# Attention tails of two head pairs: their products with v as 64 more columns of the neighbouring units' products

## The chip, the core and the metric

One core of a Trainium2 chip runs the kernel. The metric is the device time of one launch in microseconds (us), as the median over runs. The engines that matter are TensorE (PE, with its weight loads shown as PEld), VectorE (DVE), ScalarE (ACT), GpSimd (POOL) and SyncE (SP, which issues the DMAs).

## The reference

Inputs: q, k, v of 4 batches x 8 heads x 576 positions x 64, all float32. Rotary embedding is applied to q and k, then ordinary softmax attention:

```
scores = scale * q_rot @ k_rot^T          # 576 x 576 per head
attn   = exp(scores - rowmax) / (rowsum + 1e-9)
out    = attn @ v                         # 576 x 64 per head
```

The heads' outputs are laid side by side (4 x 576 x 512) and go through two feed-forward layers. The first mixes each row with the one before it, takes `relu(xk @ w_k)`, squares it, multiplies by `w_v` and gates with a sigmoid of `xr @ w_r`. The second takes `relu(x @ w_in)`, normalises one half, multiplies it with a 576 x 576 spatial matrix, gates the other half and multiplies by `w_out`.

## The kernel before

**Pairs, units and tails.** Two heads form a pair i, stacked on the 128 partitions (head 0 on partitions 0 to 63, head 1 on 64 to 127). There are 16 pairs, 4 per batch. The 576 queries of a pair are four chunks c of 128 and a rest of 64. A unit m is one pass of scores, softmax and transposes. Two pairs (a group g) make nine units: k = 0 to 3 are chunks 0 to 3 of the pair 2g, k = 5 to 8 the chunks of the pair 2g+1, and k = 4 is the tail: the last 64 queries of both pairs at once, with both heads of a pair stacked on the partitions. So the tails are the units 4, 13, 22, 31, 40, 49, 58 and 67 of 72.

**One unit.** `scores` writes two PSUM tiles (L337 for the first batch in float32, L329 and, for tails, L326 afterwards in three float32r terms). `top` takes the row maximum on DVE (L341), `expo` the exponential and the row sum on ACT (L346), `total` (L350, ACT) and `norm` (L353, DVE) the reciprocal of the sum. The scores of unit m+1 wait for both exponentials of unit m, since there is one set of score tiles.

**Turns.** For the products with v the weights must lie with the keys on the partitions. `turn(n)` transposes on PE with the identity: n = 0 and 1 are 512 keys each of the two heads (L382), n = 2 is the last 64 keys of both (L384) and, as a second tile, the reciprocals spread over 64 columns by `spread` (L357, ACT; L385, PE). `take(n)` copies the result from PSUM into the tile pt (L395; n = 0 and 1 on ACT, n = 2 on DVE).

**Products with v.** Two units in a row share a pt of 256 columns, a "duo". `values` multiplies them with v (L408): five key chunks x two heads, the heads in the left and right 64 columns of the array. `gather` multiplies the result with the turned reciprocals into the rows xt of the pair (L421, DVE).

**Tails before.** A tail has a duo of its own. `scaled` (DVE) multiplies the exponentials with the reciprocals (L363), and copies the last keys into a tile pe (L365). The turns of a tail wait for it (L374 for the 512 keys, L378 for pe). `values` then makes twenty products of 64 columns, ten for each pair, and two copies on DVE (L419) put the result into xt.

**The rest around it.** Of each finished batch, `feed` makes the products with w_k (mk, L506) and w_v (mv, L545), in twelve-matmul pieces, while the next batch's units run; each mv result is copied by ACT to a tile vs (L551) and stored by a DMA. During the first 18 units there is no finished batch. Weights are unpacked by DVE, ACT and POOL (L156 to L174) alongside. After the last unit the rest of the feed and the later layers follow (L681, L745).

**Order.** All this is entered as steps with an engine, a cost, predecessors and a rank. `Plan.order` builds one list per engine from these numbers and `emit` issues the instructions in that order, so each engine runs a fixed queue:

```
t, s = min((x for x in ready if x[0] <= soon), key=lambda x: (x[1].rank - ..., x[0]))
if best is None or t < best[0]:
    best = t, s
```

SP's queue, too, is such a list: the loads of v (L294), q and k (L246), weights (L151) and the stores. Buffers are counted by constants: VB tiles of v, PTB of pt, VSB of vs.

Of the kernel before, what the change touches and what calls it, by code (L numbers as in the profile page):

```python
# [7 lines left out]
F32 = mybir.dt.float32  # L8
# [4 lines left out]
ALU = mybir.AluOpType  # L13
# [3 lines left out]
B, H, S, D = 4, 8, 576, 64  # L17
# [7 lines left out]
NFIRST = 2  # L25
EXACT = NP
WB, GB, WB2, GB2 = 3, 2, 3, 2
RAW, ROT, VB, PFB, PTB, XTS = 2, 4, 3, 3, 2, 6
KB, RLB, VSB = 4, 2, 2
EARLY, EVERY = 24, 2.9  # L30
WAIT, SWITCH, BONUS = 0.3, 0.1, 0.0
SIDES = slice(0, HALF), slice(HALF, S)
HEAD = slice(0, 64), slice(64, 128)
# [17 lines left out]
class Plan:  # L51
# [5 lines left out]
    def add(self, eng, us, fn, deps=(), rank=0.0, after=0.12, take=None, give=None, port=False, kind=None):  # L57
        s = Step(eng, us, fn, deps, rank, after, take, give, port, kind)
        self.steps.append(s)
        return s  # L60
# [44 lines left out]
def body(ctx: ExitStack, tc, qp, kp, vp, cs, mu_k, mu_r, w_k, w_v, w_r, w_in, w_sp, b_sp, w_out, out):  # L105
    nc = tc.nc
# [10 lines left out]
    at = att.enter_context(tc.tile_pool(name="att", bufs=1, side="right"))  # L117
# [10 lines left out]
    ident = const.tile([128, 128], F32, name="ident")  # L128
# [77 lines left out]
    add = plan.add  # L206

    def which(m):
        g, w = divmod(m, 9)
        return [(2 * g, 4), (2 * g + 1, 4)] if w == 4 else [(2 * g + w // 5, w % 5 if w < 4 else w - 5)]  # L210

    ropes, vloads, exps, turned, valued, xdone, stored = {}, {}, {}, {}, {}, {}, {}
    qk, vt, xt = {}, {}, {}
# [89 lines left out]
    units, scored, duos, freed = {}, {}, {}, {}  # L303

    def unit(m):
        w = which(m)
        tail = len(w) == 2
        st = units[m] = {}
        g, k = divmod(m, 9)
        part = 0 if tail else (k - (k > 4)) % 2  # L310
        duo = duos.setdefault(5 * g + (k // 2 if k < 4 else 2 if tail else 3 + (k - 5) // 2), {"ev": [], "n": 0})
        duo["n"] = 5 * g + (k // 2 if k < 4 else 2 if tail else 3 + (k - 5) // 2)

        def scores(halves=(0, 1)):
            if 0 in halves:
# [37 lines left out]
            nc.vector.reciprocal(st["sm"][:, 3, :], st["sm"][:, 2, :])  # L353

        def spread():
            st["r"] = at.tile([128, 2, D], F32, tag="rb", bufs=3, name=f"rb{m}")
            nc.scalar.copy(st["r"], st["sm"][:, 3, :].unsqueeze(2).to_broadcast([128, 2, D]))  # L357

        def scaled(u):
            p, r = st["p"][:, u, :], st["sm"][:, 3, u:u + 1]  # L360
            if u == 0:
                st["e"] = at.tile([128, 2, 128], F32, tag="pe", name=f"pe{m}")
            nc.vector.tensor_scalar(p, p, r, None, op0=ALU.mult)  # L363
            for j in range(2):
                nc.vector.tensor_copy(st["e"][:, u, HEAD[j]], p[:, 512 - 512 * j:576 - 512 * j])  # L365

        def turn(n, slot):
            pt = st["t", n] = ps_t.tile([128, 4, 128], F32, tag=f"t{slot}", name=f"t{m}_{n}")
            p = st["p"]
            if tail and n < 2:  # L370
                for u in range(2):
                    for c in range(4):
                        k = 64 * n + 128 * c
                        nc.tensor.transpose(pt.rearrange("p c (h q) -> p (c h) q", h=2)[:, 4 * u + c, :],  # L374
                                            p[HEAD[n], u, k:k + 128], ident[HEAD[n], HEAD[n]])
            elif tail:
                for u in range(2):
                    nc.tensor.transpose(pt[:, u, :], st["e"][:, u, :], ident)  # L378
            elif n < 2:
                for c in range(4):  # L380
                    k = 64 * n + 128 * c
                    nc.tensor.transpose(pt[:, c, :], p[:, n, k:k + 128], ident)  # L382
            else:
                nc.tensor.transpose(pt[:, 0, :], p.rearrange("p a b -> p (a b)")[:, 512:640], ident)  # L384
                nc.tensor.transpose(pt[:, 1, :], st["r"].rearrange("p a b -> p (a b)"), ident)  # L385

        def take(n, eng):
            if "pt" not in duo:
                duo["pt"] = at.tile([128, 10, 256], F32, tag="pt", bufs=PTB, name=f"pt{m}")
            x = st["t", n] if n < 2 else st["t", n][:, 0:2, :]  # L390
            if tail and n < 2:
                o, x = duo["pt"][:, 0:8, HEAD[n]], x.rearrange("p c (h q) -> p (c h) q", h=2)
            else:
                o = duo["pt"][:, 4 * n:min(4 * n + 4, 10), 128 * part:128 * part + 128]
            nc.scalar.copy(o, x) if eng == "ACT" else nc.vector.tensor_copy(o, x)  # L395

        def values(slot):
            pv = duo["v"] = ps_m.tile([128, 512], F32, tag=f"m{slot}", name=f"v{m}")
            pt = duo["pt"]
            for u, (i, _) in enumerate(w):  # L400
                v = vt[i]
                for c in range(5):
                    for j in range(2):
                        if tail:
                            o, a = pv[HEAD[j], 64 * u:64 * u + 64], pt[:, 4 * u + c if c < 4 else 8 + u, HEAD[j]]
                        else:
                            o, a = pv[HEAD[j], 0:256], pt[:, 4 * j + c if c < 4 else 8, :]
                        nc.tensor.matmul(o, v[:, 4 * j + c if c < 4 else 8 + j, :], a, start=c == 0, stop=c == 4)  # L408

        def rows(i):  # L410
            if i not in xt:
                xt[i] = moe.tile([128, S + 1], F32, tag="xt", bufs=XTS, name=f"xt{i}")
                nc.gpsimd.memset(xt[i][:, 0:1], 0.0)
            return xt[i]

        def gather(u=0):
            i, c = w[u]
            if tail:
                nc.vector.tensor_copy(rows(i)[:, 513:577], duo["v"][:, 64 * u:64 * u + 64])  # L419
            else:  # L420
                nc.vector.tensor_tensor(rows(i)[:, 128 * c - 127:129 + 128 * c], duo["v"][:, 0:256], duo["pt"][:, 9, :],  # L421
                                        op=ALU.mult)

        def store(i):
            b, p = divmod(i, NP)
# [9 lines left out]
                             m - 0.5)  # L435
        t = add("ACT", 0.2, total, [exps[m, 1]], m - 0.3)
        nm = add("DVE", 0.17, norm, [t], m - 0.3)
        if tail:
            sc = [add("DVE", 0.9, lambda u=u: scaled(u), [nm, turned.get((m - 9, 2))], m - 0.25, port=True) for u in range(2)]
            ready = [sc] * 3  # L440
        else:
            ready = [[exps[m, 0]], [exps[m, 1]], [add("ACT", 0.26, spread, [nm], m - 0.3)]]
        ev = duo["ev"]
        for n in range(3):
            turned[m, n] = add("PE", (0.44, 0.44, 0.22)[n], lambda slot, n=n: turn(n, slot), ready[n], m + 0.1 * n, take="t", kind="t")
            eng = ("ACT", "ACT", "DVE")[n]
            ev.append(add(eng, (0.59, 0.59, 0.42)[n], lambda n=n, eng=eng: take(n, eng),
                          [turned[m, n]] + freed.get(duo["n"] - PTB, []), m - 0.2, give=turned[m, n]))
        if tail or part:
            v = add("PE", 1.1 if tail else 2.2, values, ev + [vloads[i] for i, _ in w], m + 0.9, take="m", kind="v")  # L450
            for u, (i, c) in enumerate(w):
                valued[i] = v
                xdone[i, c] = add("DVE", 0.2 if tail else 0.42, lambda u=u: gather(u), [v] + mixed.get(i - XTS, []), m + 0.5,
                                  give=v if u + 1 == len(w) else None)
                freed.setdefault(duo["n"], []).append(xdone[i, c])
        if m % 9 in (4, 8):
            i = 2 * (m // 9) + (m % 9 == 8)
            stored[i] = add("SP", 0.4, lambda: store(i), [xdone[i, c] for c in (1, 3, 4)], m + 1, 3)

    mixed, kept, mo = {}, {}, {}  # L460
# [122 lines left out]
    for c in range(16):  # L583
        k = c < 8
# [5 lines left out]
    for m in range(NU):  # L590
        for i, _ in which(m):
            while i not in ropes:
                prep(len(vloads))
        unit(m)
        for n, args in enumerate(early):
            if m == EARLY + int(EVERY * n):
                weight_steps(weight_early(*args), m + 12, [scored[m]])
        for i in range(B * NP):
            if i not in ropes and i >= ROT // 2 and max(which_last(i - ROT // 2)) <= m:
                prep(i)  # L600
        if m % 18 == 17:
            if m == NU - 1:
                second["close"] = close = add("SP", 0.0, lambda: open_second(), [x for x in plan.steps if x not in fed], 74, 0.1)
            n = len(plan.steps)
            for h in range(2):
                feed(m // 18, h)
            fed.update(plan.steps[n:])
# [294 lines left out]
```

## Time and profile before

| | |
|---|---|
| median of 3 runs | 787.35 us (787.33 to 789.11) |
| the profiled execution | 788.41 us, span 786.3 us |
| mean granted TensorE clock | 0.989 |
| PE busy | 750.9 us (96%) |
| DVE busy | 492.2 us (63%) |
| ACT busy | 459.0 us (58%) |

The attention units run from about 7 to 460 us of the span, the rest of the kernel behind them. A busy PE is not PE at its peak, so the order of work and the waits are read from the chain of waits and the timeline.

### The profile page before, as it was taken

To read this page: it belongs to the slowest core of one execution; us is meant where nothing else is said; L and a number is where in the kernel's file an instruction comes from. 1 tells how busy PE (TensorE), PEld (TensorE's weight loads), DVE (VectorE), ACT (ScalarE), POOL (GpSimd) and SP (SyncE) were. 2 spreads that over 40 slices of the span, in tenths; PEclk is the share of its full clock that TensorE was granted. 3 is DMA by queue.
4 is the path that set the end of the run, shared out by engine and by line. 5 is a ranking of instruction groups with operands and counts; after the bars stand their busy time and mean duration, and the time that the engine had idled before them with its cause. 6 is when DMAs were issued, how large, how long until landed. Compare 5 with 4: busy or idle time off the path is not lost.

```text
span 786.3 us, 14710 instructions
## 1 busy us (share of the span) xinstructions
PE 750.9 (96%) x5904; PEld 662.4 (84%) x5904; DVE 492.2 (63%) x937; ACT 459.0 (58%) x1037; POOL 110.6 (14%) x132
## 2 busy tenths in 40 slices
PE   4888899899999999999999998999999999999997
PEld 2555568689888888888888797998989999998997
DVE  5978998788877977977956526336553342635111
ACT  3678797677877877778876645335432432533211
POOL 1332133302111111112011100002010000101000
PEclk9989999799999999999999999999999999999999
DMA  8354432242551362352431147163201212010101
GB/s 307 119 169 146 127 118 76 90 152 99 165 173 69 140 190 77 124 178 82 134 112 55 58 156 290 46 208 116 77 15 46 76 31 91 16 31 1 61 2 60
DMA packets 35269, 84.14 MB, mean 107 GB/s; under 512 B 4545, under 2 KB 10433, under 8 KB 35202
## 3 DMA queue, kind: packets, MB, share of 16 engines
q1 hardware_dynamic: 34658, 82.63, 31.6%
q8 instruction: 46, 0.75, 0.4%
q10 hardware_dynamic: 544, 0.59, 0.2%
q14 instruction: 21, 0.17, 0.1%
HBM read 60.65 MB, written 22.55 MB: 106 GB/s over the span
## 4 chain that ended last, share of the span: by engine, by line
PE 90%; ACT 4%; DVE 3%; DMA 2%; issue 1%; SPq 1%; ACTq 0%; DVEq 0%
PE mv L545 13%; PE v L408 11%; PE mk L506 11%; PE t L382 9%; PE sp L681 8%; PE u L681 7%; PE r L681 6%; PE hv L745 6%; PE o L681 6%; PE s L329 6%; PE s L337 3%; ACT pf L346 2%; PE s L326 1%; ACT pt L395 1%; DMA wi<-wd 1%; PE t L385 1%
## 5 line engine op out<-in xcount | busy, mean ns | idle before, releaser
L341 DVE TENSOR_REDUCE sm<-s 128x1 f32<-128x576 f32 x144 | 106.4, 750 | 32.3 <-PE s L329 23.4
L346 ACT ACTIVATE pf<-s,sm 128x576 f32<-128x576 f32 x144 | 106.7, 743 | 15.1 <-DVE sm L341 14.2
L506 PE MATMUL mk<-x,wk 128*128 128x288 f32 x768 | 113.4, 300 | 1.3 <-ACT rl L513 1.3
L545 PE MATMUL mv<-kh,wv 128*128 128x288 f32 x512 | 113.4, 304 | 1.2 <-ACT kh L520 1.2
L395 ACT COPY pt<-t 128x512 f32<-128x512 f32 x144 | 83.3, 583 | 47.2 <-PE t L382 38.8
L506 PEld LDWEIGHTS mk<-x,wk 128*128 128x128 f32 x768 | 103.4, 188 | 3.0 <-ACT rl L513 1.5
L382 PE MATMUL t<-ident,pf 128*128 128x128 f32 x512 | 84.1, 288 | 15.6 <-ACT pf L346 15.6
L408 PE MATMUL v<-pt,vt 128*64 128x256 f32 (+1 forms) x960 | 93.9, 338 | 0.4 <-DVE pt L395 0.4
L382 PEld LDWEIGHTS t<-ident,pf 128*128 128x128 f32 x512 | 58.0, 143 | 38.9 <-ACT pf L346 17.1
L545 PEld LDWEIGHTS mv<-kh,wv 128*128 128x128 f32 x512 | 85.4, 190 | 5.1 <-issue 3.6
L408 PEld LDWEIGHTS v<-pt,vt 128*64 128x64 f32 x960 | 56.5, 142 | 28.9 <-issue 7.4
L545 PE MATMUL mv<-kl,wv 128*128 128x288 f32 x256 | 76.3, 298 | 0.6 <-DVE kl L524 0.6
L681 PE MATMUL sp<-ws,vn 128*128 128x288 f32 x384 | 53.9, 295 | 0.0
L681 PE MATMUL o<-g,wo 128*128 128x288 f32 x384 | 52.9, 296 | 0.5 <-ACT os L804 0.5
L681 PEld LDWEIGHTS sp<-ws,vn 128*128 128x128 f32 x384 | 52.4, 188 | 0.7
L681 PEld LDWEIGHTS o<-g,wo 128*128 128x128 f32 x384 | 51.7, 188 | 1.4 <-ACT os L804 1.2
L681 PE MATMUL r<-xr,wr 128*128 128x288 f32 x384 | 52.4, 295 | 0.0
L681 PEld LDWEIGHTS r<-xr,wr 128*128 128x128 f32 x384 | 51.7, 188 | 0.3
L681 PE MATMUL u<-x,wi 128*128 128x288 f32 x384 | 52.0, 296 | 0.0
L681 PEld LDWEIGHTS u<-x,wi 128*128 128x128 f32 x384 | 51.6, 188 | 0.3
L545 PEld LDWEIGHTS mv<-kl,wv 128*128 128x128 f32 x256 | 48.8, 191 | 1.2 <-DVE kl L524 1.2
L249 DVE TENSOR_TENSOR raw<-raw,cst 128x1152 f32<-128x1152 f32 (+1 forms) x34 | 44.7, 1316 | 5.3 <-DMA raw<-kp 5.0
(348 smaller groups left out, 1199.6 us busy)
## 6 DMA issues: line engine op xcount, KB each, us to landing
raw<-kp SPq DMA_DIRECT2D x15, 576.0 KB, 3.9
raw<-qp SPq DMA_DIRECT2D x15, 576.0 KB, 4.3
vt<-vp SPq DMA_DIRECT2D x16, 320.0 KB, 4.2
xd<-xt SPq DMA_DIRECT2D x16, 288.5 KB, 4.3
vd<-vs SPq DMA_DIRECT2D x32, 144.0 KB, 1.8
v<-vd SPq DMA_DIRECT2D x16, 288.0 KB, 2.8
out<-os SPq DMA_DIRECT2D x15, 288.0 KB, 2.1
wi<-wd SPq DMA_DIRECT2D x8, 512.0 KB, 10.0
```

Of the source, the lines that this page charges most:

```text
L249: nc.vector.tensor_tensor(t["raw", k][:, :, z], t["raw", k][:, :, z], cst[:, :, z], op=ALU.mult)
L329: nc.tensor.matmul(ps[j][:, h, :HALF], t[a, 0][r, 128 * c:128 * c + 128], t[b, 1][r, x], **f)
L337: nc.tensor.matmul(o, q[r, 128 * c:min(128 * c + 128, S)], k[r, h * HALF:(h + 1) * HALF], start=True, stop=True)
L341: nc.vector.tensor_reduce(st["sm"][:, 0, j:j + 1], st["s"][j][:, :, :HALF], axis=AX.XY, op=ALU.max, negate=True)
L346: nc.scalar.activation(st["p"][:, j, :].rearrange("p (a b) -> p a b", a=2), st["s"][j][:, :, :HALF], AF.Exp, bias=st["sm"][:, 0, j:j + 1], ...
L382: nc.tensor.transpose(pt[:, c, :], p[:, n, k:k + 128], ident)
L395: nc.scalar.copy(o, x) if eng == "ACT" else nc.vector.tensor_copy(o, x)
L408: nc.tensor.matmul(o, v[:, 4 * j + c if c < 4 else 8 + j, :], a, start=c == 0, stop=c == 4)
L506: nc.tensor.matmul(ps[:, :HALF], wk[w][:, c, fc * 128:(fc + 1) * 128], a[:, c, :], start=k == 0, stop=k == 11)
L545: nc.tensor.matmul(xs["v", dc][:, :HALF], wv[w][:, fc, dc * 128:(dc + 1) * 128], a, start=k == 0, stop=k == 23)
L681: nc.tensor.matmul(ps[:, h, :HALF], w, a[:, h * HALF:(h + 1) * HALF], start=m == 0, stop=m == n - 1)
L745: nc.tensor.matmul(ps[:, :FS], x[a][:, d, c:c + 128], wi[w][:, d, FS:], start=k == 0, stop=k == 11)
```

## The change

A tail no longer has a duo and a product of its own. Its weights stay unnormalised. They are written as columns 256 to 319 of the pt of two neighbouring duos: that of the first pair's chunks 2 and 3 (units k = 2, 3) and that of the second pair's chunks 2 and 3, which now come first (k = 5, 6; `which` changes the order of the second pair's chunks to 2, 3, 0, 1). The products of the duo (2, 3) are therefore made after the tail's turns. Two duos of four in a group are 320 columns wide, the others 256. `gather` of a wide duo multiplies 320 columns and writes chunks 2, 3 and the tail at once.

`scaled`, pe and the two copies L419 go. `spread` is called for tails too. The tail's n = 2 turn is eight float32 matmuls with the identity, 64 x 64 each (last keys, then reciprocals; two pairs; two heads), head 0 in the upper left and head 1 in the lower right quadrant of the array. A tail's `take` is two copies instead of one, into the two pt. pt tiles grow from 256 to 320 columns and have a fixed buffer each; VB goes from 3 to 2, VSB from 2 to 1 and the tile of spread reciprocals from 3 to 2. The planner's costs for these steps change.

```diff
-RAW, ROT, VB, PFB, PTB, XTS = 2, 4, 3, 3, 2, 6
-KB, RLB, VSB = 4, 2, 2
+RAW, ROT, VB, PFB, PTB, XTS = 2, 4, 2, 3, 2, 6
+KB, RLB, VSB = 4, 2, 1
...
-        return [(2 * g, 4), (2 * g + 1, 4)] if w == 4 else [(2 * g + w // 5, w % 5 if w < 4 else w - 5)]
+        return [(2 * g, 4), (2 * g + 1, 4)] if w == 4 else [(2 * g + w // 5, w if w < 4 else (w - 3) % 4)]
...
-        duo = duos.setdefault(5 * g + (k // 2 if k < 4 else 2 if tail else 3 + (k - 5) // 2), {"ev": [], "n": 0})
-        duo["n"] = 5 * g + (k // 2 if k < 4 else 2 if tail else 3 + (k - 5) // 2)
+        into = [duos.setdefault(n, {"ev": [], "n": n, "cols": 320 if n % 4 in (1, 2) else 256})
+                for n in ((4 * g + 1, 4 * g + 2) if tail else (4 * g + (k - (k > 4)) // 2,))]
+        duo = into[0]
...
-        def scaled(u):
-            p, r = st["p"][:, u, :], st["sm"][:, 3, u:u + 1]
-            if u == 0:
-                st["e"] = at.tile([128, 2, 128], F32, tag="pe", name=f"pe{m}")
-            nc.vector.tensor_scalar(p, p, r, None, op0=ALU.mult)
-            for j in range(2):
-                nc.vector.tensor_copy(st["e"][:, u, HEAD[j]], p[:, 512 - 512 * j:576 - 512 * j])
...
                 for u in range(2):
-                    nc.tensor.transpose(pt[:, u, :], st["e"][:, u, :], ident)
+                    for k in range(2):
+                        for j, r in enumerate(HEAD):
+                            nc.tensor.matmul(pt[r, u, HEAD[k]], st["r"][r, u, :] if k else p[r, u, 512 - 512 * j:576 - 512 * j],
+                                             ident[r, r], start=True, stop=True)
...
+            pt, v, z = duo["pt"], vt[w[0][0]], slice(0, duo["cols"])
+            for c in range(5):
+                for j in range(2):
+                    nc.tensor.matmul(pv[HEAD[j], z], v[:, 4 * j + c if c < 4 else 8 + j, :],
+                                     pt[:, 4 * j + c if c < 4 else 8, z], start=c == 0, stop=c == 4)
...
+        sp = add("ACT", 0.26, spread, [nm], m - 0.3)
+        ready = [[exps[m, 0], exps[m, 1]] if tail else [exps[m, 0]], [exps[m, 1]], [sp]]
         for n in range(3):
-            turned[m, n] = add("PE", (0.44, 0.44, 0.22)[n], lambda slot, n=n: turn(n, slot), ready[n], m + 0.1 * n, take="t", kind="t")
+            turned[m, n] = add("PE", (0.5, 0.5, 0.8)[n] if tail else (0.44, 0.44, 0.22)[n], lambda slot, n=n: turn(n, slot),
+                               ready[n], m + 0.1 * n, take="t", kind="t")
...
-        if tail or part:
-            v = add("PE", 1.1 if tail else 2.2, values, ev + [vloads[i] for i, _ in w], m + 0.9, take="m", kind="v")
...
+        if part and k != 3 or tail:
+            v = add("PE", 2.9 if duo["cols"] > 256 else 2.3, values, duo["ev"] + [vloads[w[0][0]]], m + 0.9, take="m", kind="v")
```

## Rows read from the trace of the kernel before

**Rows 1.** The page: busy time per engine; the copy out of PSUM; the stores of vs.

```profile
PE 750.9 (96%) x5904; PEld 662.4 (84%) x5904; DVE 492.2 (63%) x937; ACT 459.0 (58%) x1037; POOL 110.6 (14%) x132
...
L395 ACT COPY pt<-t 128x512 f32<-128x512 f32 x144 | 83.3, 583 | 47.2 <-PE t L382 38.8
...
vd<-vs SPq DMA_DIRECT2D x32, 144.0 KB, 1.8
```

**Rows 2.** Waits of PE, 20 to 160 us: total, times, longest.

```profile
PE t L382 <- ACT pf L346: 11.0, 9, 2.2
PE t L374 <- DVE pf L363: 1.8, 3, 1.2
```

**Rows 3.** Chain of waits, later stages: start, duration, what.

```profile
200.51 0.80 PE t L374 x16
...
203.10 0.22 PE t L378 x2
...
252.96 2.31 PE v L408 x20
...
261.44 1.32 PE v L408 x40
...
504.78 12.70 PE mv L545 x96
```

**Rows 4.** Chain of waits around units 4 and 13, same columns.

```profile
29.60 2.09 PE s L337 x16
...
32.49 2.84 PE v L408 x20
...
40.83 1.11 PE t L382 x4
41.95 2.33 PE v L408 x40
44.28 1.82 PE s L337 x8
...
80.07 2.85 PE v L408 x20
```

**Rows 5.** Timeline around units 4 and 13.

```profile
33.65 0.74 ACT L346 ACTIVATE pf<-s,sm 128x576 f32<-128x576 f32 x1
...
81.96 0.73 ACT L346 ACTIVATE pf<-s,sm 128x576 f32<-128x576 f32 x1
...
88.90 1.24 PE L337 MATMUL s<-rot,rot 64*128 64x288 f32 x8
```

**Rows 6.** Stretches of 1 us: PE, PEld, DVE, ACT, POOL busy; PEclk; DMA.

```profile
44.00:45.00 1.00, 1.00 (x10) 0.74 (x8) 0.36 (x2) 0.00 (x0) 0.81 (x2) 0.50 0.91 353
...
145.00:146.00 1.00, 0.79 (x5) 0.63 (x6) 1.00 (x2) 1.00 (x5) 0.09 (x1) 0.50 0.00 0
```

**Rows 7.** Timeline around unit 22 (in brackets: idle before, releaser).

```profile
131.01 1.22 DVE L363 TENSOR_SCALAR pf<-pf,sm 128x576 f32<-128x576 f32 x1
...
140.56 0.43 PE L329 MATMUL s<-rh,rl 64*128 64x288 f32 x4
...
142.31 0.75 DVE L341 TENSOR_REDUCE sm<-s 128x1 f32<-128x576 f32 x1
...
143.97 0.66 PE L382 MATMUL t<-ident,pf 128*128 128x128 f32 x4 [2.17 <-ACT pf L346]
```

**Rows 8.** Chain of waits behind unit 22.

```profile
145.38 1.81 PE s L329 x11
...
149.57 2.88 PE mv L545 x12
152.45 3.48 PE v L408 x20
...
158.15 0.99 PE s L329 x12
```

**Rows 9.** Timeline around unit 31, where nothing disturbs.

```profile
197.91 0.51 DVE L363 TENSOR_SCALAR pf<-pf,sm 128x576 f32<-128x576 f32 x1
```

More of the change, by code (lines that the diff above doesn't have):

```diff
@@ L355, in spread @@
         def spread():
-            st["r"] = at.tile([128, 2, D], F32, tag="rb", bufs=3, name=f"rb{m}")
+            st["r"] = at.tile([128, 2, D], F32, tag="rb", bufs=2, name=f"rb{m}")
             nc.scalar.copy(st["r"], st["sm"][:, 3, :].unsqueeze(2).to_broadcast([128, 2, D]))
-        def scaled(u):
-            p, r = st["p"][:, u, :], st["sm"][:, 3, u:u + 1]
-            if u == 0:
-                st["e"] = at.tile([128, 2, 128], F32, tag="pe", name=f"pe{m}")
-            nc.vector.tensor_scalar(p, p, r, None, op0=ALU.mult)
-            for j in range(2):
-                nc.vector.tensor_copy(st["e"][:, u, HEAD[j]], p[:, 512 - 512 * j:576 - 512 * j])
         def turn(n, slot):
@@ L387, in take @@
         def take(n, eng):
[L388 to L395, printed above, removed]
+            for u, d in enumerate(into):
+                if "pt" not in d:
+                    d["pt"] = at.tile([128, 10, 320], F32, tag=f"pt{d['n'] % PTB}", name=f"pt{d['n']}")
+                o = d["pt"][:, 4 * n:min(4 * n + 4, 10), 256:320]
+                if not tail:
+                    o, x = d["pt"][:, 4 * n:min(4 * n + 4, 10), 128 * part:128 * part + 128], st["t", n]
+                    x = x if n < 2 else x[:, 0:2, :]
+                elif n < 2:
+                    x = st["t", n].rearrange("p c (h q) -> p (c h) q", h=2)[:, 4 * u:4 * u + 4, :]
+                else:
+                    x = st["t", n][:, u, :].rearrange("p (h q) -> p h q", h=2)
+                nc.scalar.copy(o, x) if eng == "ACT" else nc.vector.tensor_copy(o, x)
         def values(slot):
             pv = duo["v"] = ps_m.tile([128, 512], F32, tag=f"m{slot}", name=f"v{m}")
[L399 to L408, printed above, removed]
+            pt, v, z = duo["pt"], vt[w[0][0]], slice(0, duo["cols"])
[3 more added lines that the diff above has]
+                                     pt[:, 4 * j + c if c < 4 else 8, z], start=c == 0, stop=c == 4)
         def rows(i):
@@ L414, in rows, with gather @@
             return xt[i]
[L416 to L422, printed above, removed]
+        def gather():
+            i, c = w[0][0], 128 * (duo["n"] % 4 in (1, 2))
+            z = slice(0, duo["cols"])
+            nc.vector.tensor_tensor(rows(i)[:, 1 + 2 * c:1 + 2 * c + duo["cols"]], duo["v"][:, z], duo["pt"][:, 9, z], op=ALU.mult)
         def store(i):
@@ L437, in unit @@
         nm = add("DVE", 0.17, norm, [t], m - 0.3)
[L438 to L443, printed above, removed]
+        sp = add("ACT", 0.26, spread, [nm], m - 0.3)
+        ready = [[exps[m, 0], exps[m, 1]] if tail else [exps[m, 0]], [exps[m, 1]], [sp]]
@@ L444, in unit @@
         for n in range(3):
-            turned[m, n] = add("PE", (0.44, 0.44, 0.22)[n], lambda slot, n=n: turn(n, slot), ready[n], m + 0.1 * n, take="t", kind="t")
+            turned[m, n] = add("PE", (0.5, 0.5, 0.8)[n] if tail else (0.44, 0.44, 0.22)[n], lambda slot, n=n: turn(n, slot),
+                               ready[n], m + 0.1 * n, take="t", kind="t")
             eng = ("ACT", "ACT", "DVE")[n]
-            ev.append(add(eng, (0.59, 0.59, 0.42)[n], lambda n=n, eng=eng: take(n, eng),
-                          [turned[m, n]] + freed.get(duo["n"] - PTB, []), m - 0.2, give=turned[m, n]))
@@ L449, in unit @@
-        if tail or part:
-            v = add("PE", 1.1 if tail else 2.2, values, ev + [vloads[i] for i, _ in w], m + 0.9, take="m", kind="v")
[L451 to L455, printed above, removed]
+            x = add(eng, ((0.68, 0.68, 0.55) if tail else (0.59, 0.59, 0.42))[n], lambda n=n, eng=eng: take(n, eng),
+                    [turned[m, n]] + [y for d in into for y in freed.get(d["n"] - PTB, [])], m - 0.2, give=turned[m, n])
@@ new lines, in unit @@
+            for d in into:
+                d["ev"].append(x)
+        if part and k != 3 or tail:
+            v = add("PE", 2.9 if duo["cols"] > 256 else 2.3, values, duo["ev"] + [vloads[w[0][0]]], m + 0.9, take="m", kind="v")
+            i = w[0][0]
+            valued[i] = v
+            x = add("DVE", 0.49 if duo["cols"] > 256 else 0.42, gather, [v] + mixed.get(i - XTS, []), m + 0.5, give=v)
+            freed.setdefault(duo["n"], []).append(x)
+            for c in (3, 4) if duo["cols"] > 256 else (1,):
+                xdone[i, c] = x
```

## The prediction

> **What bounds the kernel now.** I read the page first. PE is busy for 96% of the span, DVE and ACT for some 60% [rows 1]. So PE's own time decides in most places, and the question is where it does not. The list of PE's waits answers that: between 20 and 160 us the turns wait 11.0 us for exponentials and 1.8 us for `scaled` [rows 2]. Behind that the chain of waits consists of PE pieces laid end to end up to the last unit, but for one hole near 437 us. There are thus two stages. In the early one, with the tails 4, 13 and 22, PE waits for the softmax loop (scores, maximum on DVE, exponential on ACT, next scores). In the later one, with the tails 31 to 67, only PE's own work counts, and what DVE saves is worth nothing.
>
> The third thing to see is TensorE's clock. Around units 4 and 22 the granted clock falls to 0.50, that is 1.2 GHz [rows 6]. Before unit 22's fall PE had stood still for 2.17 us, waiting for an exponential [rows 7]; before unit 4's it had stood for up to 1.2 us at a time behind `scaled` [rows 2]. The pieces then take longer: at unit 22 scores take 1.81 instead of 0.99 us [rows 8], and products with v 3.48 instead of 2.31 [rows 8, 3].
>
> **PE's work for a tail.** The tail's own product goes: 40 records of 64 columns, 1.32 us, and the two transposes of pe, 0.22 us [rows 3]. Two of the four products of a group get 64 more columns. The slope comes from the two forms that the chain has: 20 records of 256 columns (5120) in 2.31 us, 40 of 64 (2560) in 1.32 us, so 0.39 ns for a column and a fixed 0.33 us for a block. 20 records of 320 columns are 6400, 1280 more, thus +0.50 us each. The bound above is plain proportion, 2.31 x 320 / 256 = 2.89, +0.58 us.
>
> The new n = 2 turn has eight float32 matmuls. A float32 matmul is two records here (a product of ten matmuls shows 20), so 16 records of 64 columns, in two quadrants by turns. The trace of before does not show this form. From below: the tails' scores of the first batch do run in quadrants, 16 records of 288 columns in 2.09 us [rows 4], or 0.13 us a record, which is 0.029 us for 64 columns and 0.47 us for 16 records. From above: if the quadrants don't overlap, the nearest row is the 16 transposes of 64 columns, 0.80 us [rows 3], and I allow 0.95. The 40 records of the tail's product, alike in columns and pairing, run at 0.033 us each, so 0.53 us for 16; this is nearest in kind and I take it.
>
> Per tail: 2 x 0.50 - 1.32 + 0.53 - 0.22 = -0.01 us. At the upper ends it is 2 x 0.58 - 1.32 + 0.95 - 0.22 = +0.57, at the lower -0.07. For the five late tails, where this is the whole effect, I take 0, from -0.4 to +2.9 us. Merging saves a block, but the columns and the new turn take it back.
>
> One rule speaks against that 0.53. The trace first: 64-column records pass at 0.033 us each in the tail's product [rows 3]. The Trainium skill, "TensorE: Matmul & The Clock Gate", Back-to-back issue gap, says that a matmul of at most 64 columns is bound by issue, at 25 ns, or at 62 ns where the sequencer decodes in software. At 62 ns the turn would be 16 x 0.062 = 0.99 us, 0.46 more than I take, 8 x 0.46 = 3.7 us over all tails. The row denies the 62 ns for this kernel, and the 25 ns changes nothing.
>
> **DVE and ACT.** DVE loses two `scaled` of 0.51 us [rows 9], which took up to 1.22 us beside POOL's work [rows 7], with four copies to pe and two L419 copies. It gains only a second small copy per tail and 64 columns in two gathers. At unit 22, where DVE is late, this counts; afterwards PE hides it. ACT gets four 256-column copies for two of 512, which take 0.583 us [rows 1]. A copy of half the columns costs between half of that and all of it, so a tail gains 0 to 1.2 us; I take the middle, 0.6, and 0.3 for the spread, which the planner enters at 0.26. Without idle time on ACT that would be 8 x 0.9 = 7.2 us. ACT is 58% busy [rows 1], and the idle time before these very copies, 47.2 us in all, is mostly a wait for PE, so I cost it at nothing, up to 0.9 us for each early tail.
>
> **Buffers and queues.** With one vs tile, ACT's copy of an mv result waits for the last store; behind it in ACT's queue stand exponentials. But four mv products need 12.70 us even when nothing lies between them [rows 3], 3.2 us each, and a store lands after 1.8 us [rows 1]: nothing. A v tile is now waited for one pair later, yet it has several units until its product; SP's list is ordered by the same predecessors, so I cost it at nothing too, some 1 us if a later load in SP's queue is held up. The copies of unit k = 7 now wait for the gather of the wide duo (2, 3); that product is made right behind the tail, two units earlier.
>
> **Unit 4.** Now: scores from 29.60, next but one scores from 44.28 [rows 4], 14.7 us for two units. The wide product must now come behind the tail's turns, and in the first batch there is no feed work to put in its place. PE has nothing between the end of unit 3's turns, 32.49 [rows 4], and the tail's second exponential, 33.65 + 0.74 = 34.39 [rows 5]: a hole of 1.9 us. Then turn, scores of unit 5, two turns, the wide product of 2.84 + 0.50 = 3.3 us less what overlaps: 34.4 + 0.4 (half of the 16 transposes [rows 3]) + 1.2 [rows 5] + 0.4 + 0.5 = 36.9, the copies some 0.8 later, the product until 41.0. Scores of unit 6 come at 41.0 instead of 44.28, -3.3, and are not slowed, (1.82 - 1.24) = -0.6 [rows 4, 5]: -3.9 us. If the clock falls after this hole as it did before, I give back what it costs now: 1.11 / 2 = 0.55 for the turns, 2.33 - 1.32 = 1.01 for the product, 1.82 - 1.24 = 0.58 for the scores [rows 3 to 5], 2.1 us. That leaves -1.8. Which of the two the hole brings the rows don't say; it is longer than the single waits of now, so I take the halving.
>
> **Unit 13.** The clock is full here now. The hole runs from 80.07 [rows 4] to 81.96 + 0.73 = 82.69 [rows 5], 2.6 us, more than the 2.17 that halved the clock at unit 22. The same sequence from 82.7 puts the next scores but one at 82.7 + 0.4 + 1.2 + 0.9 + 0.8 + 3.3 = 89.3, with a little waiting 89.5, instead of 88.90 [rows 5]: +0.6 us, and +2.1 for a halved clock: +2.7.
>
> **Unit 22.** Scores of unit 24 end at 140.56 + 0.43 = 140.99, DVE's first maximum starts only at 142.31, 1.3 us late, and PE waits 2.17 us [rows 7]. DVE has dragged along a delay since the two `scaled` (131.01). Without some 2 us of its work the maximum comes 1.3 us earlier, the hole shrinks to 0.9, and the product moved behind the tail helps to fill it. With a full clock 1.81 - 0.99 = 0.8 come back in the scores, 2.88 - 12.70 / 8 = 1.3 in mv (twelve of 96 matmuls) and 3.48 - 2.31 = 1.2 in the product [rows 8, 3], 3.3 us. Sum -1.3 - 3.3 = -4.6; bounds 0 (the hole only moves) and -5.5 (all 2.2 go).
>
> **The sum.** Unit 4 -1.8, unit 13 +2.7, unit 22 -4.6, late tails 0: -3.7 us against the profiled execution's 788.41 (span 786.3 and 2.1 around it), 784.7. That execution lies 1.06 above the median of 787.35; from the median it is 783.6 us.
>
> **Rivals.**
> *Only late work counts; no change* (25%). The hole behind unit 22 moves to another unit and the clock falls there: without the -4.6 it is +0.9, 788.3; with half of it 786.0. For it: nine waits for exponentials are spread over the early stage [rows 2]. Against it: the one of 2.17 us is the longest, and its DVE delay has a cause that goes.
> *Slower through the displaced product* (20%). Units 4 and 13 lose the product that covered their softmax. If each hole halves the clock at unit 22's price, 3.3 us, instead of 2.1, and unit 22 keeps its own, it is (-3.9 + 3.3) + (0.6 + 3.3) = +3.3, 790.7. It decides from the point where two halvings cost 2.9 us each and unit 22 gains nothing (-3.3 + 2 x 2.9 = +2.5). For it: 1.9 and 2.6 us lie on both sides of 2.17. Against it: before, PE stood nearly as idle around unit 4.
> *A slow quadrant turn* is the upper bound of PE's work: +0.57 x 8 = +4.6 against -3.7, 788.3. At the 62 ns of the Trainium skill, "TensorE: Matmul & The Clock Gate", it would be -3.7 + 3.7, 787.4, no change; I give this 5%, inside the 25, since the row runs at half of that.
>
> **How the numbers follow.** A measurement here tells no change from 0.3%, 2.4 us, so faster ends at 785.0. My forecast has 55%, 783.6, its own range 778 to 785: below, no halving at unit 4 or 13 (each -2.1) and the rest of the hole at unit 22 (-0.9). Faster 0.55, same 0.25, slower 0.20. The range for 8 in 10 takes in no change and half of the slower cases: 778.0 to 790.5.
>
> **What would show it.** Right: L363, L365, L419 and L374's wait gone; 20 wide records in about 2.8 us and the n = 2 turn in about 0.5; PE idle 1.9 to 2.6 us at units 4 and 13 before the tail's turns; no 0.50 clock near 145 us; pieces end to end later. Wrong: a turn of 0.9 us, a clock still falling in the second hundred microseconds, waits of ACT for a vs store, or PE waiting for exponentials after 160 us.

## The result and the profile after

The change makes the kernel faster: 777.68 us (777.13 to 779.48, 4 runs) against 788.23 (787.33 to 789.61, 4 runs), ratio 0.9869 [0.9844, 0.9893]. I had forecast 783.6 and a range from 778.0: the sign is right, but the gain is 10.5 us where 3.7 were forecast, and the time lies just outside the range. The profiled execution took 777.82 us (span 776.0, mean granted clock 0.998); before it was 788.41 (786.3, 0.989).

The page of the changed kernel, the lines that answer to [rows 1], and the matmuls of mk:

```profile
PE 740.8 (95%) x5696; PEld 649.9 (84%) x5696; DVE 481.0 (62%) x881; ACT 463.6 (60%) x1061; POOL 112.2 (14%) x132
...
L498 PE MATMUL mk<-x,wk 128*128 128x288 f32 x768 | 110.2, 298 | 0.4 <-ACT rl L505 0.4
L395 ACT COPY pt<-t 128x512 f32<-128x512 f32 (+1 forms) x160 | 84.8, 542 | 34.3 <-PE t L378 32.0
```

PE is busy for 10.1 us less. The instructions that went cannot explain that alone: the sum above puts a late tail at 0. Part of it is the same work at a higher clock. The matmuls of mk, which the change does not touch, took 113.4 us before and take 110.2 now:

```profile
L506 PE MATMUL mk<-x,wk 128*128 128x288 f32 x768 | 113.4, 300 | 1.3 <-ACT rl L513 1.3
```

The waits of PE from 20 to 160 us, to be read against [rows 2]:

```profile
PE t L378 <- ACT pf L347: 11.0, 10, 1.2
PE t L367 <- ACT pf L347: 3.3, 4, 1.2
```

In total PE waits no less for exponentials and scalings than before, 14.3 us against 12.8. But the longest wait is 1.2 us where it was 2.2. From 160 to 460 us no wait at all is listed; before there was one of 1.8 us. Behind 460 us there is a new one, for the last copy into vs:

```profile
PE r L673 <- ACT vs L543: 1.2, 1, 1.2
```

Where the time went is seen by the start of the same work in both chains (start, duration, what). First after: the first wide product, scores of units 6 and 7, the second wide product; then scores of unit 31, a tail's end, scores of unit 67, the last product of the units, and the first of `r` behind them.

```profile
38.44 2.84 PE v L402 x20
41.28 1.17 PE s L338 x8
...
45.11 1.43 PE s L338 x7
47.34 3.36 PE v L402 x20
...
182.10 1.60 PE s L327 x12
...
190.97 0.61 PE t L373 x16
191.59 2.84 PE v L402 x20
...
411.46 1.60 PE s L327 x12
...
446.12 2.33 PE v L402 x20
...
504.84 1.75 DMA vd<-vs
...
507.14 0.94 PE r L673 x5
```

The same work in the chain of before (scores of unit 6 stand in [rows 4]):

```profile
48.75 1.44 PE s L337 x7
50.99 2.83 PE v L408 x20
...
191.76 1.60 PE s L326 x12
...
421.24 1.60 PE s L326 x12
...
458.19 2.33 PE v L408 x20
...
517.47 1.59 PE r L681 x12
```

The lead is 9.66 us at unit 31, 9.78 at unit 67, 12.07 at the end of the units and 10.33 at `r`; so it stays to the end (spans 786.3 - 776.0 = 10.3). Smaller steps in the early stage: scores of unit 6 start at 41.28 instead of 44.28 (-3.0), those of unit 15 at 86.11 instead of 88.90 (-2.8, [rows 5]), the tail's scores of unit 22 at 122.31 instead of 124.03 (-1.7). In the timelines, first after:

```profile
86.11 1.24 PE L338 MATMUL s<-rot,rot 64*128 64x288 f32 x8
...
122.31 0.42 PE L327 MATMUL s<-rh,qe 128*128 128x288 f32 x2
```

and before:

```profile
124.03 0.51 PE L326 MATMUL s<-rh,qe 128*128 128x288 f32 x2
```

At unit 22 and at unit 31 both kernels have made the same matmuls of `feed` (48 of mk; then 156 of mk and 96 of mv), so the lead compares equal work. So unit 22 and what follows it give 7.9 us, and the late tails nothing.

Stretches of 8 us around unit 22 (PE, PEld, DVE, ACT, POOL busy; clock; DMA), before:

```profile
140.00:148.00 8.00, 5.62 (x38) 4.45 (x39) 7.55 (x12) 5.36 (x12) 6.29 (x5) 0.78 0.45 143
148.00:156.00 8.00, 7.34 (x37) 5.09 (x36) 4.38 (x7) 4.72 (x12) 0.00 (x0) 0.58 0.19 64
```

and after:

```profile
138.00:146.00 8.00, 7.52 (x64) 6.84 (x61) 6.71 (x14) 5.90 (x15) 0.00 (x0) 1.00 0.68 216
146.00:154.00 8.00, 8.00 (x65) 6.01 (x64) 6.97 (x15) 6.61 (x19) 0.00 (x0) 1.00 0.48 169
```

PE stood idle for 3.04 us of these 16 before (2.38 + 0.66) and for 0.48 after, 2.6 less. The fall to 1.2 GHz took at most (0.22 + 0.42) x 8 = 5.1 us of full-speed work from it, now nothing. 2.6 + 5.1 = 7.7 is about the 7.9 us.

### The profile page after: what moved, and what is told of

Read it like the earlier page. It is cut to its first block, busy times and chain, and to the rows that moved or that the text cites. A ratio compares the mean times of both kernels' runs of the same rounds, so it can differ in the third digit from the quotient of the medians.

```text
span 776.0 us, 14283 instructions
## 1 busy us (share of the span) xinstructions
PE 740.8 (95%) x5696; PEld 649.9 (84%) x5696; DVE 481.0 (62%) x881; ACT 463.6 (60%) x1061; POOL 112.2 (14%) x132
## 4 chain that ended last, share of the span: by engine, by line
PE 88%; DVE 4%; ACT 3%; DMA 3%; issue 0%; SPq 0%; ACTq 0%
PE mv L537 13%; PE mk L498 11%; PE v L402 11%; PE t L378 9%; PE sp L673 8%; PE r L673 7%; PE u L673 7%; PE hv L737 6%; PE o L673 6%; PE s L330 6%; PE s L338 3%; ACT pf L347 1%; DVE raw L249 1%; DMA wi<-wd 1%; PE s L327 1%; DVE sm L342 1%
## 5 line engine op out<-in xcount | busy, mean ns | idle before, releaser
L498 PE MATMUL mk<-x,wk 128*128 128x288 f32 x768 | 110.2, 298 | 0.4 <-ACT rl L505 0.4
L395 ACT COPY pt<-t 128x512 f32<-128x512 f32 (+1 forms) x160 | 84.8, 542 | 34.3 <-PE t L378 32.0
L378 PE MATMUL t<-ident,pf 128*128 128x128 f32 x512 | 82.5, 284 | 14.0 <-ACT pf L347 14.0
L402 PE MATMUL v<-pt,vt 128*64 128x256 f32 (+1 forms) x640 | 87.5, 411 | 0.0
L402 PEld LDWEIGHTS v<-pt,vt 128*64 128x64 f32 x640 | 44.3, 136 | 31.7 <-issue 4.1
```

The lines of the kernel that those rows point to most:

```text
L402: nc.tensor.matmul(pv[HEAD[j], z], v[:, 4 * j + c if c < 4 else 8 + j, :], pt[:, 4 * j + c if c < 4 else 8, z], start=c == 0, stop=c == 4)
L498: nc.tensor.matmul(ps[:, :HALF], wk[w][:, c, fc * 128:(fc + 1) * 128], a[:, c, :], start=k == 0, stop=k == 11)
```

## The experiments

All times beside runs of the kernel before on the same chip. The same program does not always get the same clock: 51 executions of the kernel before lie between 783.2 us (mean granted clock 0.998) and 789.9 (0.987). One line through all 139 executions of the kernels here (one slope, a level for each kernel) gives 5.7 us for 0.01 of mean clock and leaves a scatter of 0.64 us. The last column is each kernel's level on it, its time against before at equal clock, with a 95% interval. What the clock itself did stands in the column ahead of it. A kernel's waits also move its clock, so the last column leaves out a part of what a change does.

| kernel | median, runs | ratio | mean clock | at equal clock |
|---|---|---|---|---|
| before | 788.1, 51 | 1 | 0.991 | 0 |
| after (with its repetition) | 778.1, 9 | 0.987, 0.988 | 0.997 | -6.0 ± 0.5 |
| e1_vs_two: two vs tiles | 778.30, 6 | 0.9901 [0.9869, 0.9933] | 0.994 | -6.7 ± 0.6 |
| e2_unnorm_own: no scaling, own product | 781.56, 6 | 0.9928 [0.9901, 0.9954] | 0.996 | -3.4 ± 0.6 |
| e3_costs_only: before, other numbers | 791.14, 12 | 1.0045 [1.0027, 1.0063] | 0.987 | +0.7 ± 0.4 |
| e4_scale_back: after, scaling back | 794.21, 6 | 1.009 [1.0064, 1.0116] | 0.984 | +2.7 ± 0.6 |
| e5_second_first: after, second pair first | 779.23, 6 | 0.9901 [0.987, 0.9931] | 0.994 | -5.9 ± 0.6 |
| e6_costs_after: after, other numbers | 782.34, 12 | 0.9943 [0.9919, 0.9967] | 0.991 | -4.3 ± 0.4 |
| e7_vs_two_costs: two vs tiles, other number | 777.59, 7 | 0.9871 [0.9843, 0.9899] | 0.996 | -6.6 ± 0.6 |
| e8_costs_before2: before, other numbers again | 791.00, 12 | 1.004 [1.0024, 1.0056] | 0.989 | +2.3 ± 0.4 |
| e9_load_only: after, DVE load added | 782.09, 6 | 0.9924 [0.9903, 0.9944] | 0.994 | -4.3 ± 0.6 |
| e11_scale_on_act: before, scaling on ACT | 787.47, 6 | 0.9993 [0.9973, 1.0013] | 0.991 | -0.2 ± 0.5 |

**Half of the change: no scaling, but a product of the tail's own.** From before:

```diff
-            nc.vector.tensor_scalar(p, p, r, None, op0=ALU.mult)
...
-            sc = [add("DVE", 0.9, lambda u=u: scaled(u), [nm, turned.get((m - 9, 2))], m - 0.25, port=True) for u in range(2)]
+        sp = add("ACT", 0.26, spread, [nm], m - 0.3)
...
-                nc.vector.tensor_copy(rows(i)[:, 513:577], duo["v"][:, 64 * u:64 * u + 64])
+                nc.vector.tensor_tensor(rows(i)[:, 513:577], duo["v"][:, 64 * u:64 * u + 64], duo["pt"][:, 8 + u, 64:128], op=ALU.mult)
```

with the quadrant turn of the change in place of the two transposes of pe.

> The kernel before with one part of the change: tails stay unnormalised, their last keys and reciprocals are turned in two quadrants, and the gather multiplies by the reciprocals; but a tail keeps its own duo and its own product of 64 columns. Theory (DVE): the gain of the early stage comes from taking the two scalings and the four copies out of DVE's queue and out of the tail's path; then most of it is here already, 779 to 783 us, full clock near 145 us, and only the 0.25 us that merging saves per tail is missing (2 us over all). Rival (displaced product): the gain comes from the product that moved behind the tail and fills PE's hole there; then this kernel stays at 785 to 789 us, with the hole and the lower clock near 145 us.

781.56 us, where before has 787.59 on the same chip: 6.0 us less without merging the products. It takes the scalings off DVE and out of the tail's chain at once. Scores of units 22, 31 and 67 in its chain:

```profile
121.33 1.60 PE s L326 x12
...
185.79 1.60 PE s L326 x12
...
419.46 1.60 PE s L326 x12
```

Against before the lead is 5.97 us at unit 31 and 1.78 at unit 67. By the sum the quadrant turn costs 0.61 - 0.22 = 0.4 us a tail [rows 3], which this kernel does not get back by saving a block; in its trace the late stage costs 4.2 us, some of it in new waits (1.4 us for exponentials). At equal clock it is 2.6 us behind the changed kernel. From unit 22 to unit 31 it takes 64.5 us, where before takes 67.5 and the changed kernel 59.5: it has 3.0 of the 7.9 us there. The longest wait stays:

```profile
PE t L377 <- ACT pf L346: 11.9, 9, 2.4
```

and the granted clock there is 0.83 from 140 to 150 us. So the time is the one that the DVE theory expected, but its gain does not come from the disappearance of unit 22's hole.

**The scaling back in the changed kernel.** The exponentials of a tail are multiplied by 1.0 on DVE, and the turns wait for it:

```diff
+            nc.vector.tensor_scalar(st["p"][:, u, :], st["p"][:, u, :], 1.0, None, op0=ALU.mult)
...
+            sc = [add("DVE", 0.9, lambda u=u: scaled(u), [nm], m - 0.25, port=True) for u in range(2)]
+            ready = [sc, sc, [sp] + sc]
```

> The changed kernel with the scalings put back as multiplications by 1.0: two DVE instructions of 576 columns per tail, between the reciprocals and the turns, as before the change; the copies to pe stay away. Theory (DVE): units 4, 13 and 22 get back the wait before the turns and most of DVE's load; PE's holes at the early tails grow to 2 to 4 us, the clock falls behind at least one of them, and the time is 783 to 789 us. Rival (displaced product): the merged product is what counts; the time stays at 777 to 780 us.

794.21, worse than before, and worse than I expected: 16 us behind the changed kernel. Where they lie is read from the scores of units 22, 31 and 67:

```profile
130.90 1.60 PE s L327 x12
...
188.60 1.60 PE s L327 x12
...
425.36 1.60 PE s L327 x12
```

From unit 22 to unit 31 this kernel takes 57.7 us. It has made one piece of mk more by unit 22 (60 matmuls instead of 48, 1.6 us), so for equal work 59.3 us: as good as the changed kernel's 59.5. The scalings stand in unit 22's chain again, and neither the hole nor the halved clock comes back there:

```profile
140.00:160.00 20.00, 19.85 (x172) 15.58 (x173) 18.79 (x35) 15.90 (x41) 2.85 (x4) 1.00 0.42 134
```

It loses ahead of unit 22, where the granted clock is 0.74 from 30 to 50 us, and behind unit 31: 236.8 us to unit 67, where the changed kernel takes 229.4. PE's waits from 160 to 460 us:

```profile
PE t L376 <- ACT pt L398: 3.5, 5, 1.3
PE t L381 <- ACT pf L347: 2.1, 4, 0.6
```

In this order the late stage waits too, 5.6 us in all, where before had 1.8. So the scaling in the chain costs this kernel much, but not at unit 22, where the change gains most; and its price in before is not shown.

**Wait or load.** Two kernels take them apart. One is the changed kernel with two DVE passes of 0.75 us for each tail that nobody waits for (their result is not used):

```diff
+            nc.vector.tensor_reduce(idle, st["p"][:, u, :], axis=AX.X, op=ALU.max)
...
+                add("DVE", 0.9, lambda u=u: look(u), [nm], m - 0.25)
```

> The changed kernel with DVE work added at the tails that nobody waits for: two maxima over 576 columns of the exponentials into a spare column, 0.75 us each, about what the two scalings and the copies to pe took, with their rank. The turns do not wait for it. Theory (load): DVE's queue at unit 22 is what counted; the hole there is 2 us or more again and the clock falls near 140 us in most executions; 782 to 787 us. Rival (path): it was the wait of the tail's turns for the scalings; load alone costs less than 2 us, 777 to 780 us. The kernel with the scalings put back, which has both, took 794.

The other is before with `scaled` and the copies to pe on ACT, where DVE is rid of them but the turns wait as they did:

```diff
-            nc.vector.tensor_scalar(p, p, r, None, op0=ALU.mult)
+            nc.scalar.mul(p, p, r)
...
-            sc = [add("DVE", 0.9, lambda u=u: scaled(u), [nm, turned.get((m - 9, 2))], m - 0.25, port=True) for u in range(2)]
+            sc = [add("ACT", 1.1, lambda u=u: scaled(u), [nm, turned.get((m - 9, 2))], m - 0.25) for u in range(2)]
```

> The kernel before with the scalings and the copies to pe moved from DVE to ACT: the tail's turns still wait for them, but DVE's queue is free of them. Theory (load): DVE was late at unit 22 because of them, so 780 to 785 us, with a hole under 1.5 us there. Rival (path): the wait stays and ACT, which stands before every exponential, is late instead; 787 to 793 us.

With the load added the changed kernel loses 3.8 us of its 10 (782.09 against the 778.30 of its repetition on the same chip), 1.8 of them at equal clock. By its time that is the low end of the load theory, but what it rests on did not come: the longest wait near unit 22 is 1.2 us, and the granted clock is 1.00 from 140 to 160 us. And it is no more than other numbers alone cost the changed kernel (below): the added steps change the order as well. Relieving DVE and keeping the wait gives nothing: 787.47. Its waits from 20 to 160 us:

```profile
PE t L382 <- ACT pf L346: 10.1, 8, 2.3
PE t L374 <- ACT pf L363: 2.4, 4, 0.9
PE t L378 <- ACT pt L395: 2.2, 3, 0.9
```

The turns wait for `scaled` on ACT as they did on DVE [rows 2], the copy of pe comes late as well, and unit 22's 2.3 us are still there. ACT got the load, so this run alone does not clear the load. The two together lean to the wait in the tail's chain as the larger part, and no more.

**Numbers alone.** The change enters other costs in the planner too. Before with the products at 2.3 and 1.3 instead of 2.2 and 1.1; before with `scaled` at 0.85 and the tail's product at 1.2; the changed kernel with 2.8 and 2.2 instead of 2.9 and 2.3.

```diff
-            v = add("PE", 1.1 if tail else 2.2, values, ev + [vloads[i] for i, _ in w], m + 0.9, take="m", kind="v")
+            v = add("PE", 1.3 if tail else 2.3, values, ev + [vloads[i] for i, _ in w], m + 0.9, take="m", kind="v")
```

> The kernel before with nothing changed but two of the planner's numbers: a product with v is entered at 2.3 us instead of 2.2, a tail's at 1.3 instead of 1.1. Theory (DVE): the order changes here and there, but DVE's load at the tails stays, and with it a hole of PE of 1 to 2.5 us behind unit 22 and a clock that falls; 785 to 791 us. Rival (order): the gain is the luck of a newly planned order, and any new numbers move the time as far; then this kernel is off by 4 us or more from the kernel before, and the clock near 145 us may be full.

> The kernel before with two other planner's numbers: a scaling entered at 0.85 us instead of 0.9 and a tail's own product at 1.2 instead of 1.1. Theory (DVE): like the other new order of the kernel before, it stays within 4 us of it, 784 to 792 us, with the clock falling once or twice by 160 us. Rival (order): a new order can give the kernel before what the change gave; 782 us or less.

```diff
-            v = add("PE", 2.9 if duo["cols"] > 256 else 2.3, values, duo["ev"] + [vloads[w[0][0]]], m + 0.9, take="m", kind="v")
+            v = add("PE", 2.8 if duo["cols"] > 256 else 2.2, values, duo["ev"] + [vloads[w[0][0]]], m + 0.9, take="m", kind="v")
```

> The changed kernel with nothing but two of the planner's numbers changed: products entered at 2.8 and 2.2 us instead of 2.9 and 2.3. Theory (DVE): the gain does not hang on one order; 776 to 781 us. Rival (order): the changed kernel's order is a lucky one and a newly planned one loses several us; 782 us or more.

Neither new order of before came near the gain: 791.14 and 791.00, both slower. The changed kernel with the other numbers lost some 4 of its 10 us (782.34; 1.7 at equal clock), as the rival had it. Its PE timeline behind unit 22 has the hole of [rows 7] again:

```profile
146.58 0.66 PE L378 MATMUL t<-ident,pf 128*128 128x128 f32 x4 [2.29 <-ACT pf L347]
```

In this profile (786.96 us, clock 0.985) unit 22 to unit 31 take 62.8 us for equal work, so the hole and the clock behind it took back 3.3 of the 7.9. A larger loss lies ahead of unit 22, 5.5 us, where the granted clock is 0.83 from 30 to 50 and 0.90 from 70 to 100 us. So a part of the gain, at unit 22 and before it, depends on the order that the numbers happen to give, and on the clock of the execution.

**The hole in one piece.** The changed kernel, turning the second pair's rows first, so that a tail's turn waits for the second exponential, as I had assumed:

```diff
-                for u in range(2):
+                for u in (1, 0):
```

> The changed kernel with one loop turned round: in a tail's first two turns the second pair's transposes are issued before the first pair's, so that PE must wait for the tail's second exponential before it starts any of them, as the prediction assumed. Theory (split hole): the clock held at units 4 and 13 because the first transposes start after the first exponential and cut the hole in two (1.2 and 0.4 us); with one hole of 1.9 to 2.2 us the clock falls behind unit 4 or 13 in many executions; 779 to 784 us, mean clock 0.990 to 0.995. Rival: the length of the hole at these units does not matter for the clock, only DVE's load at unit 22 did; 777 to 779 us at a mean clock of 0.997 or more.

and the changed kernel once more, with nothing edited:

> The changed kernel itself once more, for the spread of its clock from execution to execution. Theory: it halves now and then behind units 4 and 13 as two of six executions of the kernel with two vs tiles did, whose first half is the same; times from 777 to 783 us, the slow ones at a mean clock of 0.988 to 0.995, median 778 to 780. Rival: the four executions so far show all there is; 777 to 779.5 us, mean clock at least 0.994 in each.

The line is the reversed kernel's PE at unit 4, with the hole that I had put at 1.9 us (at unit 13 it is 2.13, where I had put 2.6):

```profile
34.45 0.65 PE L367 MATMUL t<-ident,pf 64*128 64x64 f32 x7 [2.05 <-ACT pf L347]
```

779.23 us; three of its six executions have a mean clock of 0.990 to 0.994, of nine of the changed kernel one (0.994; the others 0.996 to 0.998). That leans to a short hole keeping the clock up, and no more: the first vs kernel below shows the fall behind the divided hole too. In the profile of the changed kernel's repetition (778.30, ratio 0.9876 [0.9856, 0.9896]) the fall behind units 4 and 13 did not come, and no execution fell below 0.996, as its rival had it: granted clock 1.00 from 30 to 50 and from 70 to 100 us.

**The single vs tile.** The changed kernel with two vs tiles for the last batch; and the same with the quadrant turn entered at 0.6 instead of 0.8.

```diff
-                vs = xs["vs", dc] = moe.tile([128, HALF], F32, tag="vs", bufs=VSB, name=f"vs{b}_{h}_{dc}")
+                vs = xs["vs", dc] = (second["p2"].tile([128, HALF], F32, tag="vz", bufs=2, name=f"vs{b}_{h}_{dc}") if b == B - 1 else
+                                     moe.tile([128, HALF], F32, tag="vs", bufs=VSB, name=f"vs{b}_{h}_{dc}"))
```

> The changed kernel, but in the last batch the mv results go through two vs tiles instead of one. Theory: the 1.2 us that PE stands still for ACT's copy of the last mv result before the receptance products is the price of the single tile; this kernel is 1.0 to 1.8 us faster than the changed one (776 to 777 us) and that wait is gone. Rival: the receptance products wait for something else as well (the PSUM banks of the later layers, their inputs), the wait only changes its name, and the time stays within 0.5 us of the changed kernel.

> The changed kernel with two vs tiles in the last batch, and the tail's quadrant turn entered in the planner at 0.6 us, what the trace shows, instead of 0.8. Theory: the wait for the last mv copy is worth 1.2 us and the turn's number next to nothing; 775.5 to 777.5 us, the fastest of all. Rival: a new order costs or gives more than the wait; anywhere from 774 to 781 us.

The wait of `r` is gone. The chain of the first kernel goes from mv to `r` without a store:

```profile
499.15 12.70 PE mv L537 x96
511.85 1.19 PE r L674 x9
```

In time it is 0.6 to 0.7 us at equal clock, hardly more than the intervals, where 1.2 were expected; the medians of 778.30 and 777.59 don't differ from the changed kernel's 778.1. The profiled execution of the first (782.39 us, clock 0.989) has granted clocks of 0.83 from 30 to 50 and 0.89 from 70 to 100 us, in an early order like that of the changed kernel. So the fall that I had forecast behind units 4 and 13 does come, in some executions.

## Why the prediction was right and wrong

**Right.** The two stages hold: the five late tails cost 0.0 us each (the lead is 9.66 us at unit 31 and 9.78 at unit 67). The wide product takes 2.84 us (2.81 forecast). The quadrant turn takes 0.61 us instead of 0.53, within its bounds: 0.038 us a record. The 62 ns of the issue gap in the Trainium skill, "TensorE: Matmul & The Clock Gate", Back-to-back issue gap, were weighed above record by record, and by that count this form stays below them too; a matmul of two records takes 0.076 us here, so this form alone does not deny them. The plain transposes of 64 columns do, one record each: 16 in 0.80 us, 0.050 us apiece [rows 3]. ACT's extra copies cost little and hide: two of 256 columns take 0.65 us together in the timeline, one of 512 took 0.583. At unit 4 the scores of unit 6 come 3.0 us earlier (-3.3 forecast) and those of unit 7 3.6 us (-3.9 forecast without a halved clock); from unit 6 to unit 15 the lead falls by 0.2 (+0.6 forecast for unit 13 without it).

**Wrong, the halving at units 4 and 13** (+2.1 each in the sum, 4.2 us in all). Two things failed. I let the hole run to the tail's second exponential. PE waits instruction by instruction: the first pair's transposes only need the first exponential, and the hole falls into two. PE at unit 13 after:

```profile
78.15 0.46 PE L367 MATMUL t<-ident,pf 64*128 64x64 f32 x4 [1.19 <-ACT pf L347]
79.09 0.40 PE L367 MATMUL t<-ident,pf 64*128 64x64 f32 x3 [0.47 <-ACT pf L347]
...
79.38 1.19 PE L338 MATMUL s<-rot,rot 64*128 64x288 f32 x7
```

And I made the clock a property of the order. The load experiment has the same two holes at unit 13:

```profile
79.05 0.46 PE L371 MATMUL t<-ident,pf 64*128 64x64 f32 x4 [1.19 <-ACT pf L348]
79.98 0.58 PE L371 MATMUL t<-ident,pf 64*128 64x64 f32 x3 [0.48 <-ACT pf L348]
...
80.46 2.23 PE L339 MATMUL s<-rot,rot 64*128 64x288 f32 x7
```

The same seven records of scores take 2.23 instead of 1.19 us. Two profiles with holes equal to 0.01 us differ in the clock behind them.

**Too small, unit 22** (-4.6; 7.9 measured, outside my bound of 5.5), **and its cause not borne out.** The term of the hole was 1.3 us, bounded by 2.2: 2.6 went, since the waits for `rb` (0.66) and of the scores (0.21) went with it. I had put it down to a delay that DVE drags along from the two `scaled` at 131.01. In the chain of before that leads to the hole no `scaled` stands:

```profile
135.66 1.07 ACT pt L395 x2
136.74 0.58 ACT kh L520
137.34 0.76 DVE kl L524
...
140.17 1.17 DVE I-1435_1436 L164
```

Ahead of 137.34 DVE even stood idle, waiting for ACT, and right before the late maximum it unpacks weights (L164):

```profile
137.34 0.76 DVE L524 TENSOR_TENSOR kl<-rl,kh 128x576 fp32r<-128x576 f32 x1 [0.59 <-ACT kh L520]
```

With the scalings put back into the changed kernel the hole does not return, and with other numbers it does without them. Every kernel with merged products takes 59.3 to 62.8 us from unit 22 to unit 31 for equal work, every one without 64.5 to 68.8, whether it scales or not (one profile each). So what came with the merged product, the product moved behind the tail and the order around it, goes with most of the 7.9 us; that it is the cause, and which of these, is not shown.

The term of the clock was 3.3 from three kinds of piece: the halved stretch cost up to 5.1 us, with the turns and everything else in it. Its rival, that the hole only moves, did not come about in the change's own order.

**Counted as nothing.** The hole near 437 us, 1.8 us for an exponential in before, went as well (the lead grows from 9.78 to 12.07). In the first batch the second wide product of a group takes 3.36 us where 2.83 stood before; it stood in no term of units 4 and 13. The first, which I had put at 3.3, takes 2.84. The single vs tile does cost something: stores of the last mv results are waited for, and `r` starts 1.2 us late (the last wait shown above). I had reckoned with the mean distance of mv products and not with the last ones, behind which PE has nothing else. Between the units and `r` 1.7 of the lead go; the rest of it coincides with a clock of 0.91 from 470 to 490 us, where before had 1.00 in its profile.

**The clock in the sum.** I read every row from one execution of clock 0.989. Without its terms of the clock the sum is -3.3 + 0.6 - 1.3 = -4.0 us, and these terms add up to +0.3. At equal clock the change gives 6.0 us. The other 4 are the clock: 0.997 instead of 0.991 on average, 0.006 x 570 = 3.5 us. So the term that failed most is the clock's, +0.3 forecast and about -3.5 to -4 measured. Of 51 executions of before seven reached 0.997 or more; of nine of the change seven did, and none was below 0.994.

**What stays open.** Shown is that the change without merging, `scaled` off DVE and out of the tail's chain, already gives 6.0 us, and that moving `scaled` to ACT gives none. Not shown is that these are 6.0 of the change's own 10: the two kernels gain in different places, at unit 22 3.0 against 7.9 us. How much of the rest is merging (at equal clock 2.6 us, near the 2 worked out) and how much the order can't be settled: numbers alone shift a kernel by 0.7 to 2.3 us at equal clock. Why the clock falls behind a hole in one execution and not in the next isn't settled. The merged product with the old place in the order, and v with two tiles instead of three, were not tried by themselves.

## What to carry to other kernels

In a stage that waits for a chain over several engines, an operation in that chain can cost more than its duration: 16 scalings, 8.9 us in all, cost the changed kernel 16 us when they were put back. It shifts the order and the holes, and behind a hole the clock may fall. Before blaming an operation for a hole, follow the chain back from the hole and see whether it stands there. Read what each instruction of a step waits for, not what the step waits for. And before explaining a few microseconds, compare executions at the same mean clock: here one program spans 6.7 us, nearly all of it along that line.

## What the runs showed of the hardware

The same program, run again, got mean granted clocks from 0.986 to 0.998, and its time followed with 5.7 us for 0.01. The falls to 1.2 GHz come mostly at the same places (between 30 and 50, 70 and 110, 140 and 160, and 470 and 490 us), the early ones behind idle times of 0.4 to 2.4 us, but not in each execution. A form not seen before, float32 64 x 64 matmuls with the identity in two quadrants by turns, runs at 0.038 us a record, two records for each matmul.
